# First weight load split by heads, and a narrower last output piece, in a two-block attention kernel

## The chip, the core and the metric

The kernel runs on one core of a Trainium2 chip. The metric is the device time of one execution in microseconds (us), measured several times; 343.19 us is the median before the change. A profile of one execution stands beside it. Its span, from the first to the last recorded instruction, is 341.3 us.

The engines of the core have short names in the profile: PE is TensorE (matrix multiplication), PEld its weight loads, DVE is VectorE, ACT is ScalarE, POOL is GpSimd, SP is SyncE, which here issues most of the transfers. A name with a q behind it (SPq, ACTq) is the issuing of a transfer by that engine.

## The reference, cut to what matters

Two independent attention blocks, A and B, of equal shapes; their outputs stand side by side.

```python
B, Sq, D = 16, 32, 1024
Hq, Hkv, Sk, Dh = 32, 4, 512, 128        # all arrays are bfloat16

def block(x, k_cache, v_cache, wq, wo):   # once for A, once for B
    rep = Hq // Hkv
    q = (x @ wq).reshape(B, Sq, Hq, Dh).transpose(0, 2, 1, 3)
    k = jnp.repeat(k_cache, rep, axis=1)
    v = jnp.repeat(v_cache, rep, axis=1)
    scores = jnp.einsum("bhqd,bhkd->bhqk", q, k) * (Dh ** -0.5)
    p = softmax(scores, axis=-1)
    o = jnp.einsum("bhqk,bhkd->bhqd", p, v)
    return o.transpose(0, 2, 1, 3).reshape(B, Sq, Hq * Dh) @ wo

out = jnp.concatenate([a, b], axis=-1)    # 16 x 32 x 2048
```

The 16 x 32 rows of x are 512 tokens. In the kernel they are four tiles (TT = 4) of 128 tokens. The inner dimension D = 1024 is eight chunks (DC = 8) of 128 rows.

## The kernel before

The kernel has three stages that overlap: the query projections of A and B, the attention of 128 pairs of batch and key head, and the output projections. A stream of projection matmuls is threaded through the attention so that TensorE always has something to do. The change touches the very beginning and the very end.

At the beginning nothing is in the core yet. x has to be transposed before it can be multiplied. Its first four chunks are transposed on TensorE, its last four by the transfer. The first eight heads of A are projected from weights that come in chunks; six of them (NF = 6) run first, since only six accumulators are free.

```python
NF = REP - 2          # 6 heads first, of REP = 8
HC = DC // 2
...
def load_x(d0, t0, t1, eng=nc.sync):               # two chunks of x for token tiles t0..t1
    eng.dma_start(out=x_sb[:, t0:t1, d0 * P:(d0 + 2) * P],
                  in_=x_v[:, t0:t1, d0 * P:(d0 + 2) * P])
...
def load_w0(d0, d1, h0, h1):                       # weight chunks d0..d1 for heads h0..h1
    nc.sync.dma_start(
        out=w0[d0 // HC][:, d0 % HC:(d1 - 1) % HC + 1, h0 * DH:h1 * DH],
        in_=wq_v[:, d0:d1, h0 * DH:h1 * DH])

load_x(0, TT // 2, TT, nc.scalar)
nc.scalar.preload_act_table_set("natural_log_exp_and_others")
load_x(0, 0, TT // 2)
load_w0(0, 1, 0, NF)
load_w0(1, 2, 0, NF)
load_x(2, 0, TT // 2)
load_x(2, TT // 2, TT)
load_w0(2, 3, 0, NF)
load_w0(3, 4, 0, NF)
load_w0(0, HC, NF, REP)
...
def first_heads(heads, dcs, t0=0, t1=TT):
    ts = slice(t0 * P, t1 * P)
    for dc in dcs:
        for h in heads:
            nc.tensor.matmul(first_q[h][:, ts],
                lhsT=w0[dc // HC][:, dc % HC, h * DH:(h + 1) * DH],
                rhs=xT[0][:, dc, ts],
                start=(dc == 0 and t0 == 0), stop=(dc == DC - 1))

warm_up(22)                                        # matmuls on constants while x is loaded
for k, ts in enumerate(((0, TT // 2), (TT // 2, TT))):
    transpose_x(0, *ts, nc.vector.tensor_copy)     # 128x128 transposes, then a copy to SBUF
    transpose_x(1, *ts, nc.scalar.copy, spare[k])
first_heads(range(NF), (0,))
first_heads(range(0, NF - 2), (1,))
transpose_x(2, 0, TT, nc.vector.tensor_copy)
transpose_x(3, 0, TT, nc.scalar.copy)
first_heads(range(NF - 2, NF), (1,))
first_heads(range(NF), (2, 3))
...
```

At the end the last token tile of B is projected in three pieces of the 1024 output columns. Each piece is 32 matmuls (one for each head) into one PSUM tile, a copy to SBUF, and a store.

```python
def f_units(pr, tt, n0, width, eng):
    ps = psum.tile([P, NW], FP32, name="f_ps", tag="proj")     # NW = 512
    nh, off = divmod(n0, NW)
    for h in range(HQ):
        nc.tensor.matmul(ps[:, 0:width], lhsT=oT[pr, tt][:, h, :],
            rhs=wo_tiles[pr, nh, h // REP][:, h % REP, off:off + width],
            start=(h == 0), stop=(h == HQ - 1))
        if h == HQ - 1:
            o_sb = outp.tile([P, NW], BF16, name="o_sb")
            nc.scalar.copy(out=o_sb[:, 0:width], in_=ps[:, 0:width])
            c0 = problems[pr][5] + n0
            eng.dma_start(out=out_flat[tt * P:(tt + 1) * P, c0:c0 + width],
                          in_=o_sb[:, 0:width])
        yield
...
    yield from f_units(1, TT - 1, 0, NW, nc.sync)
    yield from f_units(1, TT - 1, NW, QW, nc.sync)             # QW = 256
    yield from f_units(1, TT - 1, NW + QW, QW, nc.scalar)
```

Of the kernel before, what the change touches and what calls it, by code (L numbers as in the profile page):

```python
# [16 lines left out]
P = 128  # L17
# [164 lines left out]
def kernel(  # L182
# [14 lines left out]
    nc = tc.nc  # L197
# [5 lines left out]
    TT = NTOK // P  # L203
    NOUT = D
    NW = 512
# [4 lines left out]
    QW = REP * SQ  # L210
# [7 lines left out]
    def fast_path(ok_i):  # L218
        with ExitStack() as fctx:
# [74 lines left out]
            def q_units(pr, h):  # L294
                g, hl = divmod(h, REP)
                if hl == 0:
                    qT[pr, g] = blk_tile([P, B, REP, SQ], "qT")
                w = wq_tiles[pr, h // 4]
                ps = psum.tile([P, NW], FP32, name="q_ps", tag="proj")
                for dc in range(DC):  # L300
                    nc.tensor.matmul(  # L301
                        ps[:],
                        lhsT=w[:, dc, (h % 4) * DH:(h % 4 + 1) * DH],
                        rhs=xT[pr][:, dc, :],
                        start=(dc == 0),
                        stop=(dc == DC - 1),
                    )
                    if dc == DC - 1:
                        nc.scalar.copy(  # L309
                            out=qT[pr, g][:, :, hl, :],  # L310
                            in_=ps[:].rearrange("p (b s) -> p b s", s=SQ),
                        )
                    yield

            def f_units(pr, tt, n0, width, eng):
                ps = psum.tile([P, NW], FP32, name="f_ps", tag="proj")
                nh, off = divmod(n0, NW)
                for h in range(HQ):
                    assert all((pr, b, h // REP) in normalized for b in range(tt * BPT, (tt + 1) * BPT))
                    nc.tensor.matmul(  # L320
                        ps[:, 0:width],
                        lhsT=oT[pr, tt][:, h, :],
                        rhs=wo_tiles[pr, nh, h // REP][:, h % REP, off:off + width],
                        start=(h == 0),
                        stop=(h == HQ - 1),
                    )
                    if h == HQ - 1:
                        o_sb = outp.tile([P, NW], BF16, name="o_sb")
                        nc.scalar.copy(out=o_sb[:, 0:width], in_=ps[:, 0:width])  # L329
                        c0 = problems[pr][5] + n0  # L330
                        eng.dma_start(  # L331
                            out=out_flat[tt * P:(tt + 1) * P, c0:c0 + width],
                            in_=o_sb[:, 0:width],
                        )
                    yield
# [119 lines left out]
            NF = REP - 2  # L455
# [8 lines left out]
            def load_x(d0, t0, t1, eng=nc.sync):  # L464
                eng.dma_start(
                    out=x_sb[:, t0:t1, d0 * P:(d0 + 2) * P],
                    in_=x_v[:, t0:t1, d0 * P:(d0 + 2) * P],
                )
# [7 lines left out]
            def load_w0(d0, d1, h0, h1):  # L476
                nc.sync.dma_start(
                    out=w0[d0 // HC][:, d0 % HC:(d1 - 1) % HC + 1, h0 * DH:h1 * DH],
                    in_=wq_v[:, d0:d1, h0 * DH:h1 * DH],
                )  # L480
# [1 line left out]
            load_x(0, TT // 2, TT, nc.scalar)  # L482
            nc.scalar.preload_act_table_set("natural_log_exp_and_others")
            load_x(0, 0, TT // 2)
            load_w0(0, 1, 0, NF)
            load_w0(1, 2, 0, NF)
            load_x(2, 0, TT // 2)
            load_x(2, TT // 2, TT)
            load_w0(2, 3, 0, NF)
            load_w0(3, 4, 0, NF)  # L490
            load_w0(0, HC, NF, REP)
# [28 lines left out]
            def transpose_x(d, t0, t1, copy, ps=None):  # L520
                if ps is None:
                    ps = psum.tile([P, NTOK], BF16, name="xT_ps", tag="ob")
                for tt in range(t0, t1):
                    nc.tensor.transpose(  # L524
                        ps[:, tt * P:(tt + 1) * P], x_sb[:, tt, d * P:(d + 1) * P], ident[:]
                    )
                ts = slice(t0 * P, t1 * P)
                copy(out=xT[0][:, d, ts], in_=ps[:, ts])  # L528
# [5 lines that stand above are left out]
                        nc.tensor.matmul(  # L534
                            first_q[h][:, ts],
                            lhsT=w0[dc // HC][:, dc % HC, h * DH:(h + 1) * DH],
                            rhs=xT[0][:, dc, ts],
                            start=(dc == 0 and t0 == 0),
                            stop=(dc == DC - 1),
                        )  # L540

            warm_up(22)
            for k, ts in enumerate(((0, TT // 2), (TT // 2, TT))):
                transpose_x(0, *ts, nc.vector.tensor_copy)
                transpose_x(1, *ts, nc.scalar.copy, spare[k])
            first_heads(range(NF), (0,))
            first_heads(range(0, NF - 2), (1,))
            transpose_x(2, 0, TT, nc.vector.tensor_copy)
            transpose_x(3, 0, TT, nc.scalar.copy)
# [5 lines left out]
            for n, h in enumerate((0, 2, 4, 6, 5, 7, 1, 3)):  # L555
                first_heads((h,), (DC - 1,))
                copy = nc.vector.tensor_copy if n % 2 else nc.scalar.copy
                copy(  # L558
                    out=qT[0, 0][:, :, h, :],
                    in_=first_q[h].rearrange("p (b s) -> p b s", s=SQ),  # L560
                )

            def stream():
                for h in range(REP, HQ):
                    yield from q_units(0, h)
                for h in range(HQ):
                    yield from q_units(1, h)
                for nh in range(NH):
                    for tt in range(TT):
                        yield from f_units(0, tt, nh * NW, NW, nc.gpsimd)  # L570
                for tts in ((0, 1), (2,)):
                    for nh in range(NH):
                        for tt in tts:
                            yield from f_units(1, tt, nh * NW, NW, nc.sync)
                yield from f_units(1, TT - 1, 0, NW, nc.sync)
                yield from f_units(1, TT - 1, NW, QW, nc.sync)
                yield from f_units(1, TT - 1, NW + QW, QW, nc.scalar)

            units = stream()
            run(units, 2 * DC)  # L580

# [70 lines left out]
            for k, (lim, op) in enumerate(((1.0 / SUM_HI, ALU.is_ge), (1.0 / SUM_LO, ALU.is_le))):  # L652
                nc.vector.tensor_scalar(
                    out=flags, in0=rall[0:QD].rearrange("p j n -> p (j n)"),
# [18 lines left out]
    ok_i = flag.tile([1, 1], I32, name="ok_i")  # L673
    total = 2 * 2 * NG * QW
    ok = fast_path(ok_i)
    with tc.If(ok < total, preferred_fallthrough_block=True, label="general"):
        general_path(tc, problems, out_flat)
# [30 lines left out]
```

## Time and profile before

| what | value |
|---|---|
| time, median of 3 runs (lowest to highest) | 343.19 us (343.18 to 343.21) |
| span of the profiled execution | 341.3 us |
| TensorE busy | 337.1 us, 99% |
| VectorE busy | 265.5 us, 78% |
| ScalarE busy | 185.8 us, 54% |
| read from HBM, written | 50.86 MB, 2.10 MB |

The busy time of an engine is the sum of its instructions. For TensorE the end of a matmul is modelled, so two matmuls in a row overlap in the record; the distance from one start to the next is the better measure of what one costs. The times in a timeline count from the start of the span. In a timeline row the first number is the start, the second is how long the row lasts, x counts the instructions that were merged into it, and the bracket at the end tells how long the engine was idle before it and what ended that wait.

### The profile page before, as it was taken

The numbers are of one execution on the slowest core, as the hardware profiler recorded it, in microseconds if no ns is written. First come the engines' busy times: TensorE is split into PE (matmuls) and PEld (weight loads), VectorE is DVE, ScalarE is ACT, GpSimd is POOL, SyncE is SP. The second block draws the span as 40 slices with busy tenths as digits, with TensorE's granted clock in tenths as the row PEclk, the third lists the DMA queues.
The fourth block names the chain that finished last, engine by engine and source line by source line (L and its number), as shares of the span: only waits on it lengthen the run. The fifth ranks groups of instructions, "written<-read, shape, count | busy, mean of one in ns | idle before, by whom it ended". The sixth has DMA issues, their size and how long they took to land.

```text
span 341.3 us, 5487 instructions
## 1 busy us (share of the span) xinstructions
PE 337.1 (99%) x2118; PEld 213.2 (62%) x2118; DVE 265.5 (78%) x336; ACT 185.8 (54%) x209; POOL 46.6 (14%) x206
## 2 busy tenths in 40 slices
PE   8999999999999999999999999999999999999996
PEld 6455666666666666666666666666666666666555
DVE  1046988888988898888888988879888888889540
ACT  3058666666667667666645545555555555555110
POOL 0001110011111111110012221222122101111100
PEclk9999999999999999999999999999999999999999
DMA  6999999889999988999999985999449997440001
GB/s 188 294 179 274 295 245 219 200 222 260 303 282 170 232 231 229 212 239 325 287 272 281 265 189 141 332 242 270 121 103 316 354 164 180 100 105 12 18 17 34
DMA packets 127966, 71.70 MB, mean 210 GB/s; under 512 B 75840, under 2 KB 127168, under 8 KB 127936
## 3 DMA queue, kind: packets, MB, share of 16 engines
q1 hardware_dynamic: 127136, 70.07, 87.6%
q0 software_dynamic: 384, 1.05, 0.8%
q8 instruction: 17, 0.28, 0.4%
q10 hardware_dynamic: 416, 0.20, 0.2%
q14 instruction: 13, 0.11, 0.1%
HBM read 50.86 MB, written 2.10 MB: 155 GB/s over the span
## 4 chain that ended last, share of the span: by engine, by line
PE 99%; ACT 0%; issue 0%; DVE 0%; ACTq 0%
PE f_ps L320 32%; PE q_ps L301 28%; PE s_ps L357 16%; PE ob L425 16%; PE q_ps L534 4%; PE q_ps L516 1%; PE xT_ps L524 0%; ACT o_sb L329 0%; DVE xT L528 0%; ACTq L329 0%
## 5 line engine op out<-in xcount | busy, mean ns | idle before, releaser
L365 ACT ACTIVATE p_sb<-s_ps,shift 128x1024 bf16<-128x1024 f32 x128 | 142.6, 1114 | 97.7 <-PE s_ps L357 86.2
L376 DVE TRANSPOSE_TENSOR_REDUCE parts<-p_sb 128x32 f32<-128x1024 bf16 x128 | 158.7, 1240 | 20.9 <-ACT p_sb L365 19.3
L320 PE MATMUL f_ps<-wo_sb,oT 128*128 128x512 bf16 (+1 forms) x544 | 132.3, 367 | 0.0
L301 PE MATMUL q_ps<-xT,wq_sb 128*128 128x512 bf16 x448 | 116.9, 379 | 0.0
L425 PE MATMUL ob<-p_sb,v_sb 128*128 128x256 bf16 x512 | 76.8, 273 | 0.0
L357 PE MATMUL s_ps<-qT,kT 128*128 128x256 bf16 x512 | 76.8, 273 | 0.0
L320 PEld LDWEIGHTS <-oT 128*128 128x128 bf16 x544 | 53.2, 98 | 35.3
L357 PEld LDWEIGHTS <-kT 128*128 128x128 bf16 x512 | 56.9, 113 | 28.3
L301 PEld LDWEIGHTS <-wq_sb 128*128 128x128 bf16 x448 | 43.8, 98 | 32.2
L425 PEld LDWEIGHTS <-v_sb 128*128 128x128 bf16 x512 | 50.1, 98 | 20.0
L447 DVE TENSOR_TENSOR oT<-r,ob 128x512 bf16<-128x512 f32 x64 | 43.9, 685 | 19.9 <-PE ob L425 19.4
L411 DVE STREAM_TRANSPOSE r<-rall 128x512 f32<-128x512 f32 x64 | 44.2, 691 | 1.1
L309 ACT CAST qT<-q_ps 128x512 bf16<-128x512 f32 x56 | 32.6, 582 | 16.6 <-PE q_ps L301 16.6
L394 POOL COPY half<-cs 64x32 f32<-64x32 f32 x32 | 6.5, 204 | 231.9 <-DVE cs L384 231.9
L329 ACT CAST o_sb<-f_ps 128x512 bf16<-128x512 f32 (+1 forms) x17 | 9.5, 558 | 23.6 <-PE f_ps L320 23.6
L534 PE MATMUL q_ps<-xT,w_sb 128*128 128x512 bf16 x64 | 14.4, 380 | 0.2 <-DVE xT L528 0.2
L384 DVE TENSOR_REDUCE cs<-parts 128x32 f32<-128x128 f32 x32 | 12.1, 377 | 1.1
L406 DVE RECIPROCAL rall<-sums 128x32 f32<-128x32 f32 x32 | 10.2, 318 | 3.3 <-POOL sums L403 3.3
L534 PEld LDWEIGHTS <-w_sb 128*128 128x128 bf16 x64 | 6.1, 98 | 7.7 <-DMA w_sb<-in_A_wq_dram 0.8
L558 DVE CAST qT<-q_ps 128x512 bf16<-128x512 f32 x4 | 2.5, 682 | 10.3 <-PE q_ps L534 10.3
L331 POOL DMA_DIRECT2D out_dram<-o_sb x8 | 4.6, 574 | 29.3 <-ACT o_sb L329 29.3
L395 POOL TENSOR_TENSOR half<-half,cs 64x32 f32<-64x32 f32 x32 | 7.8, 242 | 2.6
(25 smaller groups left out, 44.8 us busy)
## 6 DMA issues: line engine op xcount, KB each, us to landing
v_sb<-in_A_v_cache_dram SPq DMA_DIRECT2D x16, 512.0 KB, 5.8
wq_sb<-in_B_wq_dram SPq DMA_DIRECT2D x8, 1024.0 KB, 5.8
wo_sb<-in_A_wo_dram SPq DMA_DIRECT2D x8, 1024.0 KB, 7.3
v_sb<-in_B_v_cache_dram SPq DMA_DIRECT2D x16, 512.0 KB, 4.9
wo_sb<-in_B_wo_dram SPq DMA_DIRECT2D x8, 1024.0 KB, 8.5
wq_sb<-in_A_wq_dram SPq DMA_DIRECT2D x5, 1024.0 KB, 6.5
wq_sb<-in_A_wq_dram SPq DMA_DIRECT2D x2, 512.0 KB, 7.5
kT<-in_A_k_cache_dram SPq DMA_TRANSPOSE x64, 4.4
```

What stands on the lines that cost most here:

```text
L301: nc.tensor.matmul(ps[:], lhsT=w[:, dc, (h % 4) * DH:(h % 4 + 1) * DH], rhs=xT[pr][:, dc, :], start=(dc == 0), stop=(dc == DC - 1),)
L309: nc.scalar.copy(out=qT[pr, g][:, :, hl, :], in_=ps[:].rearrange("p (b s) -> p b s", s=SQ),)
L320: nc.tensor.matmul(ps[:, 0:width], lhsT=oT[pr, tt][:, h, :], rhs=wo_tiles[pr, nh, h // REP][:, h % REP, off:off + width], start=(h == 0), ...
L357: nc.tensor.matmul(s_ps[:, c, :], lhsT=kT[:, i % GRP, c, :], rhs=qT[pr, g][:, b, :, :].rearrange("p h s -> p (h s)"), start=True, stop=True,)
L365: nc.scalar.activation(out=p_sb[:], in_=s_ps[:], func=ACTF.Exp, bias=shift[:], scale=SCALE)
L376: nc.vector.tensor_reduce(out=parts[k][:, q, :, :].rearrange("p c h -> p (c h)"), in_=st[i]["p"][:].rearrange("p c (h s) -> p (c h) s", s=SQ),
L384: nc.vector.tensor_reduce(out=cs[:], in_=parts.pop(k)[:].rearrange("p q c h -> p q h c"), axis=AX.X, op=ALU.add,)
L406: nc.vector.reciprocal(out=rall[:, k, :], in_=quad.pop(k)[:])
L411: nc.vector.transpose(out=r[:].rearrange("p n s -> p (n s)"), in_=rall[:, k, o * 2 * REP:(o + 1) * 2 * REP] .unsqueeze(2).to_broadcast([P, ...
L425: nc.tensor.matmul(ob[j][:, q, :], lhsT=v_sb[:, i % GRP, c, :], rhs=st[i]["p"][:, c, :], start=(c == 0), stop=(c == KC - 1),)
L447: nc.vector.tensor_tensor(out=out, in0=rcp.pop(j)[:].rearrange("p (q h) s -> p q h s", h=REP), in1=ob.pop(j)[:].rearrange("p q (h s) -> p ...
L534: nc.tensor.matmul(first_q[h][:, ts], lhsT=w0[dc // HC][:, dc % HC, h * DH:(h + 1) * DH], rhs=xT[0][:, dc, ts], start=(dc == 0 and t0 == 0 ...
```

## The change

It has two parts.

At the beginning, the weights of the first chunk for six heads came in one load. They now come in two loads of three heads each, and the first three heads are multiplied with the first half of the tokens before the second half, so that TensorE need not wait for the whole of the load and of the transposed x. The second pair of x chunks, which came in two loads, now comes in one, so that the number of loads ahead of the third weight chunk is as before.

At the end, the last output piece is 128 columns wide and not 256, and VectorE copies it and not ScalarE. The piece ahead of it is 384 wide. This is to shorten what is left to do after the last matmul.

```diff
-            def f_units(pr, tt, n0, width, eng):
+            def f_units(pr, tt, n0, width, eng, copy=nc.scalar.copy):
...
-                        nc.scalar.copy(out=o_sb[:, 0:width], in_=ps[:, 0:width])
+                        copy(out=o_sb[:, 0:width], in_=ps[:, 0:width])
...
             load_x(0, 0, TT // 2)
-            load_w0(0, 1, 0, NF)
+            load_w0(0, 1, 0, NF // 2)
+            load_w0(0, 1, NF // 2, NF)
             load_w0(1, 2, 0, NF)
-            load_x(2, 0, TT // 2)
-            load_x(2, TT // 2, TT)
+            load_x(2, 0, TT)
             load_w0(2, 3, 0, NF)
...
-            first_heads(range(NF), (0,))
+            for ts in ((0, TT // 2), (TT // 2, TT)):
+                first_heads(range(0, NF // 2), (0,), *ts)
+            first_heads(range(NF // 2, NF), (0,))
             first_heads(range(0, NF - 2), (1,))
...
-                yield from f_units(1, TT - 1, NW, QW, nc.sync)
-                yield from f_units(1, TT - 1, NW + QW, QW, nc.scalar)
+                yield from f_units(1, TT - 1, NW, NW - P, nc.sync)
+                yield from f_units(1, TT - 1, 2 * NW - P, P, nc.scalar, nc.vector.tensor_copy)
```

## The prediction

> **What bounds the kernel now.** I read the page's busy table first, then the chain that ended last, then two short windows of the trace: the first 8 us and the last 10. The first two say why only these windows matter.
>
> ```profile
> PE 337.1 (99%) x2118; PEld 213.2 (62%) x2118; DVE 265.5 (78%) x336; ACT 185.8 (54%) x209; POOL 46.6 (14%) x206
> ...
> PE 99%; ACT 0%; issue 0%; DVE 0%; ACTq 0%
> ```
>
> TensorE is busy 99% of the 341.3 us and is 99% of the chain. About 4 us of the span are not matmuls: some 0.9 us before the first one, a few tenths of waits in the first 8 us, and 3 us after the last one. The change adds and removes no matrix work, so it can only move these 4 us. The timeline of the start:
>
> ```profile
> 1.25 0.92 SPq L477 DMA_DIRECT2D w_sb<-in_A_wq_dram  x2
> ...
> 3.21 1.97 SPq L477 DMA_DIRECT2D w_sb<-in_A_wq_dram  x4
> 3.24 1.06 PE L524 MATMUL xT_ps<-ident,x_sb 128*128 128x128 bf16 x8
> 3.70 0.72 DVE L528 COPY xT<-xT_ps 128x256 bf16<-128x256 bf16 x2 [2.74 <-PE xT_ps L524]
> ...
> 4.33 0.25 PEld L534 LDWEIGHTS <-w_sb 128*128 128x128 bf16 x2 [0.29 <-DMA w_sb<-in_A_wq_dram]
> 4.47 2.38 PE L534 MATMUL q_ps<-xT,w_sb 128*128 128x512 bf16 x10 [0.17 <-DVE xT L528]
> ...
> 6.69 0.61 PE L524 MATMUL xT_ps<-ident,x_sb 128*128 128x128 bf16 x8
> ```
>
> Two things hold the first projection matmul to 4.47: its weights (weight load at 4.33, released by a transfer) and the second half of the transposed x (0.17 us after the engine went idle). The second wait comes 3 us later. The chain in order of time, and the weight loads in the same window:
>
> ```profile
> 7.30 0.43 PE q_ps L534 x2
> 7.73 0.01 issue
> 7.74 0.61 PE q_ps L534 x2
> ```
> ```profile
> 7.74 0.33 PEld L534 LDWEIGHTS <-w_sb 128*128 128x128 bf16 x3 [0.50 <-DMA w_sb<-in_A_wq_dram]
> ```
>
> At 7.74 the first matmul of the third 128-row chunk (I call it w2) starts, released by its transfer. The two matmuls ahead of it started at 7.14 and 7.36; at 0.216 us each (52 of them fill 7.74 to 18.98, where the next line's begin) the engine was free at 7.57. So **w2's landing costs 0.17 us, and from 7.74 on nothing stops TensorE any more**. The end of the timeline:
>
> ```profile
> 334.79 0.37 ACT L329 CAST o_sb<-f_ps 128x256 bf16<-128x256 f32 x1 [2.91 <-PE f_ps L320]
> 338.29 0.37 ACT L329 CAST o_sb<-f_ps 128x256 bf16<-128x256 f32 x1 [3.12 <-PE f_ps L320]
> 338.69 0.37 ACTq L331 DMA_DIRECT2D out_dram<-o_sb  x1
> ```
>
> After the last matmul there are, one after the other: ScalarE's copy of 256 columns (0.37), the issue on its queue (338.69), the landing 1.6 us after the start of the issue (340.3), and 1.0 us of closing work to 341.3.
>
> [...] The trace's eight warm transposes, each with its own weights, take 0.61 us of which the last alone is 0.219: (0.61 - 0.22)/7 = 56 ns. [...] The last output goes from 512 B to 256 B a row; no transfer of before shows what that does to a store.
>
> **The change part by part.**
>
> *Tail, matrix work.* Two pieces of 32 matmuls with 256 columns become 32 with 384 and 32 with 128. Before: 338.29 - 334.79 = 3.50 us a piece, 109 ns each, 7.0 us for both. After: 128 columns at 56 ns, and 384 halfway between 109 and 216, 162 ns; 32 x (162 + 56) = 6.98. Change 0.0.
>
> *Tail, copy.* ScalarE took 0.372. For VectorE I scale this trace: bf16 copies from PSUM (line 528) take 292 ns at 256 columns and 425 at 512, so the fixed part is 159; the fp32 eviction of 512 columns takes 682, so (682 - 159)/512 = 1.02 ns a column, and 128 columns come to 159 + 131 = 290. [...] I take 0.28. **Change -0.09.** ScalarE at 128 would be near 0.266 by its own two sizes (372 at 256 columns, 585 at 512: 0.83 ns a column), so the gain is that of the width, and the other engine adds nothing of its own. VectorE has many more semaphores to wait for (older output transfers), but all long since satisfied; the wait for TensorE stands in the last of its waiting instructions, as on ScalarE.
>
> *Tail, store.* Rows of 256 B for 512 B: the 128 packets of the last store stand in the trace at 27 ns each, eight to a DMA engine, 0.2 us. Half the bytes may save some 0.05 there[...]. I take -0.02. The 384-wide store is issued 1.6 us before the last one (1.79 of matmuls, less 0.2 that its wider copy takes longer) and lands before it.
>
> *Head, first chunk.* The six heads' weights (192 KB, issue at 1.25, landing 3.0 us later, 4.28) come as two loads of three heads, and those three heads run on the first half of the tokens before the second half. TensorE is free of transposes at about 4.10; if the first half-load has landed by then, it starts there and not at 4.47. Three matmuls of 256 columns at the slow starting rate (128 columns take 107 ns in the warm-up, so 213) fill the gap: 4.10, 4.31, 4.52, the third partly fast already, since the first matmul of before, at 4.47, was followed after 0.28 us, between the slow 0.427 and the fast 0.216; so it ends at 4.67. Three fast ones of 109 ns and three of 216 follow: 5.65. Before, the six heads end at 6.69 - 4 x 0.216 = 5.83 (four of the ten matmuls are the second chunk's). Gain about 0.19 at this point.
>
> *Head, issue slots.* The extra weight load takes SyncE's slot of the second chunk, and the merged x load takes one slot for two: 2 + 2 loads become 3 + 1. So w2 is issued at 3.21 as before; only the second chunk is issued 0.5 later (2.2).
>
> *What becomes of the 0.19.* Before w2 the engine now waits 0.17; with 0.19 gained ahead of it, it would wait 0.36, until the same landing at 7.70 (3.21 + 4.5). The bytes ahead of w2 are the same; 128 packets of 1,536 B become 256 of 768 B, which I put at a few hundredths more. **Change 0.0**, and the gain at the first chunk is lost in a longer wait.
>
> Sum: 0.0 - 0.09 - 0.02 + 0.0 = -0.11; 343.19 - 0.11 = **343.08 us**.
>
> **The rivals.**
>
> (a) w2 lands earlier, or is not the last wait. Then up to 0.17 + 0.19 = 0.36 us are to be had, and the time is 342.72. For it: in 6.2 to 7.2 the DMA engines are only 44% busy, so the transfer isn't limited by bytes alone. Against it: issue time and bytes ahead are unchanged.
>
> (b) w2 or the second chunk lands later. The second chunk lands at 5.47 now (1.75 + 3.7) and would be wanted at 5.65; issued 0.5 later it may miss that by 0.1 or 0.2, which the slack ahead of w2 absorbs. The merged x load (the second of two lands at 2.69 + 3.5 = 6.2 now) is wanted at 6.50. Only w2 itself costs: 0.1 us late is 343.18.
>
> [...]
>
> (d) The small store lands 0.1 to 0.2 later, and eats the copy's gain: 343.2.
>
> **Range and chances.** The sure part is the copy. Half of (a) and (d) against each other span about 0.2 either way: 342.88 to 343.28. Two per cent are 6.9 us, more than all that the change touches: within 2% at 0.99, 0.005 for each side.
>
> **What would show it.** Right: the last copy on VectorE near 0.28 us; landing 1.6 us after the issue; the 32 last matmuls at 56 ns; first projection matmul near 4.1; the wait ahead of w2 grown to about 0.35 and w2's first matmul again near 7.74. Wrong: that matmul before 7.65 or after 7.85 (then the head moved the time); a copy as long as ScalarE's[...].

## The result, and the profile after

The changed kernel takes 344.26 us (median of 6 runs, 344.03 to 344.95); the kernel before, run beside it, 343.29 us (343.18 to 343.73). The ratio is 1.0029, with a 95% interval of 1.0016 to 1.0042. The change costs about 1 us, where 0.1 us less had been predicted.

The busy line of the page, and what its part 4 has for the chain that ended last:

```profile
PE 337.9 (99%) x2121; PEld 212.6 (62%) x2121; DVE 265.8 (77%) x337; ACT 185.7 (54%) x208; POOL 46.7 (14%) x206
...
DVE 0%
DVE o_sb L329 0%
```

TensorE's work is as before, plus three matmuls. The chain now has a single link, VectorE's copy. What released that copy is put down to TensorE's sequencer (PEq L678 in the timeline of the end below), and the chain breaks off there, so it says nothing of what became longer. The timeline of the start:

```profile
3.99 1.11 PEld L534 LDWEIGHTS <-w_sb 128*128 128x128 bf16 x6
4.09 1.49 PE L534 MATMUL q_ps<-xT,w_sb 128*128 128x256 bf16 x6
...
5.75 0.13 PEld L534 LDWEIGHTS <-w_sb 128*128 128x128 bf16 x2 [0.65 <-DMA w_sb<-in_A_wq_dram]
5.76 2.10 PE L534 MATMUL q_ps<-xT,w_sb 128*128 128x512 bf16 x7 [0.18 <-DMA w_sb<-in_A_wq_dram]
...
7.69 0.61 PE L524 MATMUL xT_ps<-ident,x_sb 128*128 128x128 bf16 x8
...
19.81 3.62 PE L301 MATMUL q_ps<-xT,wq_sb 128*128 128x512 bf16 x16
```

The first matmul does start at 4.09, as worked out. But the six halves run at the slow rate throughout (1.49 less the 0.42 of the last, over five, is 0.214 us each), and the fourth head then waits for the second half-load, until 5.75. The next stage starts at 19.81; before it was 18.98. The timeline of the end:

```profile
337.34 0.48 ACT L329 CAST o_sb<-f_ps 128x384 bf16<-128x384 f32 x1 [4.61 <-PE f_ps L320]
...
339.14 0.29 DVE L329 CAST o_sb<-f_ps 128x128 bf16<-128x128 f32 x1 [9.37 <-PEq L678]
339.46 0.37 ACTq L331 DMA_DIRECT2D out_dram<-o_sb  x1
```

The copy is what was expected, 0.29 us. The transfers in the window 338.5 to 342.5 (by queue: packets, MB, share of the DMA engines' time; then the store with its KB and the us from issue to landing; the rows that the profile names "instruction" are read here as fetches of program code):

```profile
q8 instruction: 1, 0.02, 1.8%
q14 instruction: 2, 0.02, 1.3%
...
out_dram<-o_sb ACTq DMA_DIRECT2D x1, 32.0 KB, 2.6
```

The store landed 2.6 us after its issue, not 1.6. So the two profiles, 341.28 and 343.05 us long, differ by these terms: the last copy starts 0.85 later (339.14 for 338.29), it is 0.08 shorter, and the store lands 1.0 later. What follows the landing is 1.0 us in both. The experiments tell which of these terms belong to the change, and which to this one profile.

### The profile page after: what moved, and what is told of

Read it like the earlier page. It is cut to its first block, busy times and chain, and to the rows that moved or that the text cites. A ratio compares the mean times of both kernels' runs of the same rounds, so it can differ in the third digit from the quotient of the medians.

```text
span 343.0 us, 5497 instructions
## 1 busy us (share of the span) xinstructions
PE 337.9 (99%) x2121; PEld 212.6 (62%) x2121; DVE 265.8 (77%) x337; ACT 185.7 (54%) x208; POOL 46.7 (14%) x206
## 5 line engine op out<-in xcount | busy, mean ns | idle before, releaser
L320 PE MATMUL f_ps<-wo_sb,oT 128*128 128x512 bf16 (+2 forms) x544 | 132.3, 366 | 0.0
L320 PEld LDWEIGHTS <-oT 128*128 128x128 bf16 x544 | 52.0, 98 | 36.7
L534 PE MATMUL q_ps<-xT,w_sb 128*128 128x512 bf16 (+1 forms) x67 | 15.4, 390 | 0.2 <-DMA w_sb<-in_A_wq_dram 0.2
L534 PEld LDWEIGHTS <-w_sb 128*128 128x128 bf16 x67 | 6.8, 104 | 8.0 <-DMA w_sb<-in_A_wq_dram 0.7
```

The source lines that it names most:

```text
L320: nc.tensor.matmul(ps[:, 0:width], lhsT=oT[pr, tt][:, h, :], rhs=wo_tiles[pr, nh, h // REP][:, h % REP, off:off + width], start=(h == 0), ...
L534: nc.tensor.matmul(first_q[h][:, ts], lhsT=w0[dc // HC][:, dc % HC, h * DH:(h + 1) * DH], rhs=xT[0][:, dc, ts], start=(dc == 0 and t0 == 0 ...
```

## The experiments

All times are medians beside runs of the kernel before on the same chip; ratios are against these, with 95% intervals. A difference of 0.3% needs many runs: single executions of one kernel spread over more than 1 us here.

**The kernel before once more, and the changed kernel once more.** No edit.

> The kernel before once more, unchanged, for the spread of its own start and end. In its first profile TensorE's matmuls turned from the slow to the fast rate at 4.6 us and the last store landed 1.6 us after its issue; in the changed kernel's profile these were 6.6 us and 2.6 us. If the hour of the turn is chance and not the change's doing, this profile may show any turn between about 4 and 7 us, with a time up to 0.9 us above 343.2 when it is late. If it belongs to the code, the turn is again at 4.6 and the time 343.2.

> The changed kernel once more. If late clock and late landing are chance, this profile shows them earlier, and the time comes down to about 343.5. If they belong to the code: turn near 6.6 us, second half-load landing near 5.7 us, time near 344.2.

Measured: before 343.44 against 343.45 us, ratio 0.9997 (0.9988 to 1.0006). Changed 344.05 against 343.45, ratio 1.0021 (1.0015 to 1.0028, 22 runs). So the loss is real. The moment at which TensorE turns to its fast rate differs between executions of the same kernel: 3.76 us in this profile of before, where the first had 4.63, and 5.24 in this one of the changed kernel, where the first had 6.63. The table at the end of this section has all of them. In the new profile of the changed kernel the last copy starts at 338.27 and not at 339.14, so the 0.85 us of the first profile is not lost every time. The late landing is:

```profile
338.27 0.29 DVE L329 CAST o_sb<-f_ps 128x128 bf16<-128x128 f32 x1 [9.37 <-PEq L678]
338.59 0.37 ACTq L331 DMA_DIRECT2D out_dram<-o_sb  x1
```
```profile
q10 hardware_dynamic: 144, 0.03, 9.9%
q14 instruction: 1, 0.01, 2.0%
...
out_dram<-o_sb ACTq DMA_DIRECT2D x1, 32.0 KB, 2.3
```

(The second fence is the transfers in the window 338.59 to 340.1.) Again 2.3 us to the landing, and again a transfer on queue 14, of instructions, beside the store's packets.

**Each half of the change alone.**

```diff
 # beginning only                         # end only
+load_w0(0, 1, 0, NF // 2)               +..., NW, NW - P, nc.sync)
+load_w0(0, 1, NF // 2, NF)              +..., 2 * NW - P, P, nc.scalar,
+load_x(2, 0, TT)                        +     nc.vector.tensor_copy)
+first_heads in two halves of tokens
```

> The beginning changed, the end as before. Theory (the beginning costs all that every run shows, the end is worth -0.1 with an occasional late landing): +0.8 to +0.9 us, a little above the whole change's best runs. Rival (the end costs about half): +0.4 us.

> The end changed, the beginning as before. Theory: -0.1 us (copy 0.29 for 0.37), landing 1.6 us after the issue. Rival (rows of 256 B land late by themselves, as in the changed kernel's profile, 2.6 us): +0.4 to +0.9 us.

Measured: beginning only 343.26 against 343.45 us, ratio 0.9994 (0.9986 to 1.0003). End only 344.23 against 343.45, ratio 1.0022 (1.0014 to 1.0031). My theory fell, and so did its numbers for both halves: the beginning costs nothing that can be measured, and the end alone loses as much as the whole change. In the profile of the end alone the store landed 2.4 us after its issue, with the copy at 0.29.

What in the end is late? Three things are new there: rows of 256 B, a narrow last piece, and VectorE as the copier. VectorE stands out in one more way. It has no other work at the end: in the kernel before it leaves this code at 329.6 us, with GpSimd (329.5), where SyncE, TensorE and ScalarE leave it at 335.6, 336.1 and 339.1. It leaves by a branch of the kernel's own, which jumps over a second, general version of the computation that did not run here:

```python
ok = fast_path(ok_i)                     # all that was shown above
with tc.If(ok < total, preferred_fallthrough_block=True, label="general"):   # L676, L678 after
    general_path(tc, problems, out_flat)
```

In the program this branch stands behind the instructions that each engine has in the fast path. What stands behind it is called the closing block here. The sequencer's records of VectorE's branch, before and after (count, duration in ns, first and last start in us):

```profile
L676 DVEq COMPARE_BRANCH  x1: 84/84/84, 329.6 to 329.6; - x1
```
```profile
L678 DVEq COMPARE_BRANCH  x1: 84/84/84, 339.2 to 339.2; - x1
```

In the trace of before two transfers of 8,192 B on queue 14 follow at 330.64 and 330.80, after the branches of GpSimd and VectorE, and a third at 340.18, 1.1 us after ScalarE's. In the changed kernel one of the first two is gone from there, and comes 1.2 to 1.5 us after VectorE's late branch (339.2 and 340.72; in the second profile 338.3 and 339.50). That is when the packets of the last store move. Which engine a fetch belongs to is read from these times; the records don't name it.

**The end with ScalarE as the copier, and VectorE as the copier at the old widths.**

```diff
 # ScalarE, 384 + 128 columns
-yield from f_units(1, TT - 1, NW, QW, nc.sync)
-yield from f_units(1, TT - 1, NW + QW, QW, nc.scalar)
+yield from f_units(1, TT - 1, NW, NW - P, nc.sync)
+yield from f_units(1, TT - 1, 2 * NW - P, P, nc.scalar)
 # VectorE, 256 + 256 columns
-yield from f_units(1, TT - 1, NW + QW, QW, nc.scalar)
+yield from f_units(1, TT - 1, NW + QW, QW, nc.scalar, nc.vector.tensor_copy)
```

> The end as changed (384, then 128 columns), but both copied by ScalarE; the beginning as before. Theory (VectorE, because it has the last copy, goes to the closing block only then, and the fetch of its instructions there shares a DMA engine with the last store): VectorE is in the closing block by 331 us again, no instruction fetch of 8,192 B falls into the store but ScalarE's own late one, the store lands 1.6 us after its issue, and the time is 0.1 us below before. Rival (rows of 256 B, or a narrow last piece that moves TensorE's own instruction fetch later, make the store late): +0.4 to +0.8 us as with VectorE.

> Widths as before (256 and 256), the last piece copied by VectorE. Theory of the fetch: landing 2.1 to 2.6 us after the issue, +0.6 to +0.8 us (the copy of 256 columns takes about 0.42 there). Rival (rows of 256 B): 512 B rows land 1.6 us after the issue, +0.05 us.

Measured: ScalarE 343.40 against 343.61 us, ratio 0.9995 (0.9987 to 1.0003). VectorE at 256 columns 344.31 against 343.61, ratio 1.0019 (1.0011 to 1.0026). The loss goes with VectorE, and not with the rows or the width. With ScalarE as the copier VectorE took its branch at 329.7 again, as before. The transfers from the issue of the store on, VectorE at 256 columns (window 339.74 to 341.3):

```profile
q10 hardware_dynamic: 144, 0.07, 14.2%
q14 instruction: 1, 0.01, 2.3%
...
out_dram<-o_sb ACTq DMA_DIRECT2D x1, 64.0 KB, 2.2
```

The store has its full rows of 512 B and lands 2.2 us after the issue. The profile of ScalarE at 128 columns was not clean either: 2.1 us to the landing, with no queue 14 among its transfers from 338.7 to 340.2 but TensorE's fetch of 16,384 B on queue 8, at 338.78 to 339.76:

```profile
338.40 0.27 ACT L329 CAST o_sb<-f_ps 128x128 bf16<-128x128 f32 x1 [1.31 <-PE f_ps L320]
338.70 0.37 ACTq L331 DMA_DIRECT2D out_dram<-o_sb  x1
```
```profile
q10 hardware_dynamic: 144, 0.03, 11.8%
q8 instruction: 1, 0.02, 4.1%
...
out_dram<-o_sb ACTq DMA_DIRECT2D x1, 32.0 KB, 2.1
```

The median says that this happens in few of its runs, or costs little; which of the two is open. ScalarE's copy of 128 columns takes 0.27 us, VectorE's 0.29, so giving the copy to the other engine had nothing to bring.

**Only VectorE's branch delayed, nothing else.** If the fetch is the cause, a kernel that stores exactly as before must get slower when VectorE is merely kept from its branch.

```diff
                         eng.dma_start(...)
+                        if late:                     # last piece only
+                            nc.vector.tensor_copy(out=scrap[:], in_=ps[:, 0:1])
```

> The kernel before, in every store and copy; VectorE only reads one column of the last accumulator besides, into a tile that nothing uses, so that it is held until then. Theory of the fetch: though nothing on the way to the end changes, the store lands 2.1 to 2.6 us after its issue, +0.5 to +0.8 us. Rival (the row size or the width): no change.

Measured: 343.44 against 343.61 us, ratio 0.9999 (0.9991 to 1.0007). The expected loss did not come. Its trace shows a reason that I had not foreseen: VectorE's copy waited for ScalarE's copy of the same accumulator, so that its branch came at 339.27, 0.42 after the start of that copy and not with it. The fetch then began at 340.46, just after the last data packet of the store had started (340.45). The landing, 1.9 us after the issue, was late by only 0.25. In this execution the fetch came too late to hold the store's data, so the run is not the test that it was meant to be; it supports the theory as little as it refutes it. The next pair puts the delay where it can be chosen.

```diff
+                    if h == hold:                    # HQ - 1, or 0, in the last piece
+                        hold_ps = psum.tile([P, NW], FP32, name="hold_ps", tag="ob")
+                        nc.tensor.matmul(hold_ps[:, 0:P], lhsT=warm, rhs=warm,
+                                         start=True, stop=True)
+                        nc.vector.tensor_copy(out=scrap[:], in_=hold_ps[:, 0:1])
```

> The kernel before, all stores and copies as they were; one small matmul on constants goes ahead of the last matmul (0.06 us), and VectorE copies one column of its result to a tile that nothing uses. So VectorE reaches its branch about 0.2 us before the last copy starts, without anything on the way to the end waiting for it. Theory (VectorE's late fetch of 8,192 B of instructions shares a DMA engine with the last store): fetch inside the store, landing 2.1 to 2.4 us after the issue, +0.5 to +0.8 us. Rival (the store is late only if VectorE feeds it, or if its rows are short): +0.06 us.

> The same small matmul and copy, ahead of the first of the last piece's 32 matmuls: VectorE reaches its branch 3.4 us before the last copy. Theory: its fetch ends long before the store, landing 1.6 us after the issue, +0.06 us. If any added VectorE work costs: as the run beside it, +0.5 or more.

Measured: ahead of the last matmul 344.12 against 343.34 us, ratio 1.0022 (1.0013 to 1.0032). Ahead of the first 343.58 against 343.34, ratio 1.0003 (0.9994 to 1.0012). The two kernels have the same instructions; only their place differs, by 31 matmuls. The timeline of the first of the two, then its transfers from the issue on (339.25 to 340.6):

```profile
338.69 0.16 DVE L325 COPY scrap<-hold_ps 128x1 f32<-128x1 f32 x1 [9.26 <-PE hold_ps L322]
338.85 0.37 ACT L336 CAST o_sb<-f_ps 128x256 bf16<-128x256 f32 x1 [3.18 <-PE f_ps L327]
339.25 0.37 ACTq L338 DMA_DIRECT2D out_dram<-o_sb  x1
```
```profile
q10 hardware_dynamic: 143, 0.07, 17.1%
q14 instruction: 1, 0.01, 2.1%
...
out_dram<-o_sb ACTq DMA_DIRECT2D x1, 64.0 KB, 2.1
```

And the second, with its transfers from 339.6 to 340.9:

```profile
335.66 0.16 DVE L325 COPY scrap<-hold_ps 128x1 f32<-128x1 f32 x1 [5.87 <-PE hold_ps L322]
...
339.20 0.37 ACT L336 CAST o_sb<-f_ps 128x256 bf16<-128x256 f32 x1 [3.18 <-PE f_ps L327]
```
```profile
q10 hardware_dynamic: 144, 0.07, 17.2%
...
out_dram<-o_sb ACTq DMA_DIRECT2D x1, 64.0 KB, 1.6
```

ScalarE's copy starts right after its last matmul in both; nothing on the way to the store waits for VectorE. With the fetch in the window the landing takes 2.1 us, without it 1.6. In the trace of the first, the fetch runs from 339.90 to 340.35; nine tenths of the store's 128 packets start by 340.39, the last at 340.58; and of its sixteen completions fifteen come by 340.88 and one at 341.32. One share of sixteen is late; the landing is that of the last completion, and the span ends 1.0 us after it, at 342.3.

**What holds that share back.** The records of single packets show when it is held, in the four profiles in which VectorE copies the last piece. In each, eight of the store's 128 data packets, one sixteenth, start 0.15 to 0.45 us after the others, one behind the other, and at the moment when the fetch ends. In the second profile of the changed kernel the fetch ends at 339.990 and the eight packets start from 339.987 on; with the end alone these are 340.252 and 340.248, with 256 columns 341.099 and 341.095, in the first profile of the changed kernel 341.032 and 341.029. The store's packets (queue 10) in the second profile of the changed kernel, of which the window 338.59 to 340.1 above has 144, are these from 339.73 to 340.12:

```profile
q10 hardware_dynamic: 9, 0.00, 2.5%
```

These nine are the eight late packets and their completion mark, and the first of them starts at 339.987. The records don't number the DMA engines, but with the two times within 4 ns of each other in all four profiles the late share is taken to run on the engine that fetches. In the kernel held to the last matmul it is not held back as a block; there its last packets take 0.05 to 0.10 us, where the others take 0.027. Two things stay open. In the first profile of the changed kernel the fetch's own record starts at 340.73 only, when the packets of the other shares had all started (340.34 to 340.58), so it does not cover all the time in which the late share was held. And wherever a fetch fell beside the store, the last completion comes 0.6 to 0.9 us after the packet of its mark, for 0.4 to 0.5 without one.

**A version without VectorE's copy, and one that keeps TensorE's fetch out of the way too.**

```diff
 # both with the changed beginning; ScalarE copies
 # 384 + 128 columns                      # 320 + 192 columns
+..., NW, NW - P, nc.sync)               +..., NW, NW - 192, nc.sync)
+..., 2 * NW - P, P, nc.scalar)          +..., 2 * NW - 192, 192, nc.scalar)
```

> The changed beginning with the end of 384 and 128 columns, all copied by ScalarE: the change without its VectorE copy. Theory: -0.2 to -0.3 us against before (0.1 from the beginning, 0.1 from the end). Rival (rows of 256 B): +0.4.

> The changed beginning, the last piece 192 wide, the one ahead 320, all copied by ScalarE. The copy comes to 0.32 us, TensorE's own fetch of 16,384 B comes earlier than with 128 columns and ends before the store. Theory: landing 1.6 us after the issue, -0.1 to -0.2 us against before, the lowest of all versions if only by a little. Rival (a narrow piece pays): above before.

Measured: 384 + 128 343.48 against 343.61 us, ratio 0.9997 (0.9989 to 1.0005); landing 1.6 us in its profile. 320 + 192 343.32 against 343.34, ratio 0.9995 (0.9986 to 1.0004); landing 1.6 us, copy 0.32. Both are well below the changed kernel's ratio of 1.0021 to 1.0029. Neither is shown to beat the kernel before, so the gains that I expected of them are not shown, and the two can't be told apart. TensorE's fetch ended before the store in both profiles (339.04 and 339.30, with the first packets of the stores at 339.31 and 339.85), so whether 192 columns keep it away where 128 do not was not put to the test.

**The loads of the beginning without the new order of matmuls.**

```diff
+load_w0(0, 1, 0, NF // 2)
+load_w0(0, 1, NF // 2, NF)
+load_x(2, 0, TT)
 first_heads(range(NF), (0,))             # as before
```

> Only the loads of the beginning are changed (first chunk in two, second x pair in one); the six heads run over all tokens in one go, as before; the end as before. In three profiles of the changed beginning the third chunk landed at 6.9 to 7.5 us and the second half of the first at 5.0 to 5.7; before it was 7.7 and 4.3. If these landings belong to the loads: the same here, a wait of 0.3 to 0.6 us at the fourth head's first matmul, and a time within 0.15 us of before. If they belong to the order of the matmuls (nothing in the transfers should know of it): landings as before.

Measured: 343.52 against 343.34 us, ratio 1.0003 (0.9996 to 1.0011). In its profile the second half of the first chunk landed at 5.48, as in the changed kernel, and the third chunk at 7.72, as before. The fourth head waited for the second half from 5.06 to 5.53, 0.47 us. So the late second half comes with the loads, whatever the order of the matmuls. The earlier third chunk was not reproduced with them.

The beginnings of all fourteen profiles, from the trace's records of the clock, the transfers' completions and the first matmul of the next stage (us). "First six heads" is the landing of the first chunk for six heads, or of its second half:

| kernel | fast rate from | first six heads | third chunk | next stage |
|---|---|---|---|---|
| before | 4.63 | 4.28 | 7.70 | 18.98 |
| before, once more | 3.76 | 4.40 | 7.74 | 19.02 |
| end only | 5.41 | 4.23 | 7.33 | 19.20 |
| end only, ScalarE | 3.84 | 4.58 | 7.81 | 19.09 |
| 256 columns, VectorE | 6.49 | 4.87 | 7.63 | 19.96 |
| VectorE held behind ScalarE's copy | 6.10 | 4.19 | 7.82 | 19.54 |
| VectorE held to the last matmul | 5.47 | 4.38 | 7.43 | 19.22 |
| VectorE held to the first matmul | 5.56 | 4.51 | 7.49 | 19.33 |
| loads only | 3.83 | 5.48 | 7.72 | 19.17 |
| changed | 6.63 | 5.71 | 7.53 | 19.81 |
| changed, once more | 5.24 | 5.01 | 6.92 | 18.95 |
| beginning only | 4.25 | 5.18 | 7.04 | 18.87 |
| beginning, 384 + 128 | 4.58 | 4.67 | 7.09 | 18.84 |
| beginning, 320 + 192 | 3.76 | 5.63 | 7.48 | 19.32 |

The turn to the fast rate lies anywhere between 3.8 and 6.6 us, with both beginnings. The three profiles with the latest turns (6.63, 6.49, 6.10) are the three with the latest next stage, two with the old beginning and one with the new.

The beginning is not all of the spread. From the next stage to the last copy most profiles take 319.31 or 319.32 us, but "before, once more" takes 319.63. TensorE waits there for weights of the next projections:

```profile
27.54 0.76 PEld L301 LDWEIGHTS <-wq_sb 128*128 128x128 bf16 x5 [0.63 <-DMA wq_sb<-in_A_wq_dram]
```

The two kernels in which VectorE is held by a small matmul have such a wait at the same place, near 27.5 us; the other eleven profiles have none.

## Why the prediction was wrong

**The step that failed** is the tail's store: "I take -0.02", and "landing 1.6 us after the issue". With it falls "the other engine adds nothing of its own". That sentence was true of the copy, which took the time expected, but I looked only at what the copy waits for, and not at what waits behind the copy in VectorE's stream: the branch over the general version, and the fetch of instructions that follows it. In the prediction the tail came to -0.11 us, from the copy and the store. Measured, the tail alone is about +0.76 (0.0022 of 343.45). The copy's saving is there, 0.08 us in the profiles. The store's term, predicted at -0.02, is +0.7 to +1.0 in the three profiles with the 128 columns on VectorE (landings at 2.3, 2.4 and 2.6 for 1.6). That is the term that the sum had wrong, and it alone carries the result out of the range.

**Why a fetch of 8 KB costs this much.** In the traces the 8,192 B on queue 14 are one packet, of 0.3 to 0.7 us, where one of the store takes 18 or 27 ns. The eight packets of the late share start within 4 ns of its end, and one completion of sixteen is late, in the kernel held to the last matmul by 0.44 us after the fifteenth. (The 16,384 B put down to TensorE stand on queue 8 in these traces.) How a DMA engine divides its time between queues was not shown; that the late share and the fetch are on one engine is my reading of the 4 ns. The pair of kernels in which only the place of VectorE's hold differs shows that the time of the branch decides: ratios 1.0022 and 1.0003, landings 2.1 and 1.6 us after the issue.

**Rival (d)** had the right symptom (the small store lands late) with the wrong cause; its 0.1 to 0.2 us was a guess of mine. Rows of 256 B landed 1.6 us after the issue in the version with the changed beginning and 384 + 128 columns on ScalarE, and rows of 512 B landed 2.1 and 2.2 us after it in the two kernels where the fetch fell beside them. No run shows a price of the 256 B rows in this store.

**The matmuls of the tail** went as predicted: in the trace of the changed kernel the 32 matmuls of 128 columns follow each other at 55 to 56 ns throughout, those of 384 at 162, and the last copy starts 1.80 us after that of the 384-wide piece (339.14 - 337.34), where 32 x 56 ns were expected to be 1.79.

**The beginning.** The first matmul at 4.09 was right. "Change 0.0" for the beginning agrees with the run, whose interval goes from -0.5 to +0.1 us, but by luck, for the way there was another. I had the gain wait ahead of an unmoved third chunk. In none of the five profiles of the changed beginning does TensorE wait there: the third chunk landed at 6.9 to 7.5, and its first matmul started at 7.6 to 8.6. So rival (a) had the path right, that w2 lands earlier and is not the last wait; its gain of 0.36 us is neither shown nor excluded. A later w2, rival (b), came in none of them. The gain goes earlier and in different ways. In three of the five the fourth head waits 0.4 to 1.0 us for the second half-load; with 384 + 128 columns on ScalarE TensorE waits 0.2 us for the second chunk instead; in the second profile of the changed kernel it waits for neither, but five of the six halves run at the slow rate, which turned at 5.24. With the old beginning, too, w2 is waited for only in the three profiles with a turn before 5 us.

The second half-load lands at 4.7 to 5.7, where the whole load of before landed at 4.2 to 4.9. Half a microsecond of this is its issue, at 1.75 for 1.25. From issue to landing it takes 2.9 to 4.0 us, for 2.9 to 3.6. What makes it vary is open: single packets of 768 B took up to 1.4 us in the trace of the changed kernel where most take 36 ns, but the trace of before has such packets too (1,536 B, up to 1.7 us where most take 65 ns).

**The range** of 0.2 us either way was too narrow for another reason. The first three runs of before, 343.18 to 343.21, looked like a spread of 0.03 us. Some fifty later ones span 342.83 to 344.04. I read the turn to the fast rate in one profile and took it for the kernel's, and wrote that from 7.74 on nothing stops TensorE: in three of the fourteen profiles weights do, near 27.5 us. In the profiles the start of the last copy differs by what happens before the next stage, by this wait and by an added matmul (0.06 us), and by nothing else above 0.02 us; how much of the spread of the times these make was not measured.

## What to carry to other kernels

This kernel ends with a branch, to jump over its general version. In the kernel before, VectorE ran out of work early and took the branch early (329.6 us), and the last store landed 1.6 us after its issue. With the very last operation given to VectorE, its branch came at 338.3 to 339.3, the fetch fell beside the last store, and the store landed 2.2 to 2.6 us after its issue. So in a kernel that ends in this way choose for the last operation an engine that is busy at the end anyway; here the issuing of the last store kept ScalarE there in any case. A kernel without such a branch was not run, so whether it has these fetches is open. And compare the stores' landings, not only the copies that feed them.

## What the runs showed of the hardware that was not expected

- The branch over the general version is followed, 1.0 to 1.6 us later, by a transfer of 8,192 B of instructions (0.3 to 0.7 us on queue 14) for VectorE, ScalarE and GpSimd, and one of 16,384 B (0.9 to 1.3 us on queue 8) for TensorE; which is whose is read from the times. Eight packets of the last store start within 4 ns of the end of VectorE's fetch, in four profiles.
- With a fetch beside them, stores of 32 and 64 KB landed 2.1 to 2.6 us after the issue, for 1.6 without; 1.9 where the fetch began just after the store's last data packet.
- TensorE's branch is recorded 2.1 us ahead of the end of its matmuls with 256 columns in the last piece (336.1 for 338.2 in the kernel before) and 1.2 us ahead with 128 (337.9 for 339.1 in the changed kernel), so with the narrower last piece its fetch came closer to the store: at 128 columns it overlapped the store in one profile of ScalarE's version, and missed it in the other.
- TensorE's turn to the fast rate, 3.8 to 6.6 us after the start, differs from run to run of the same kernel (4.63 and 3.76; 6.63 and 5.24). With the two latest turns the next stage started 0.8 and 1.0 us later than in the first profile of before.
- A copy of 128 fp32 columns out of PSUM takes 0.27 us on ScalarE and 0.29 on VectorE; of 256 columns 0.37 and 0.42.
